# Ranks of a chunk's tokens from a running sum and three matmuls in place of nine, with a new table of orders, in a recurrence and mixture-of-experts kernel

## The chip, the cores and the metric

The kernel runs on one core of a Trainium2 chip. The metric is device time in microseconds (us) of one execution. TensorE is called PE below, VectorE DVE, ScalarE ACT, GpSimd POOL, and SyncE SP; SP and ACT also issue DMAs.

## The reference

First a gated linear recurrence over 4 sequences of 5056 tokens and 256 features, then a top-1 mixture of 8 experts over all 20224 tokens, all in f32:

```python
a_t = exp(8 * sigmoid(r_gate) * log(sigmoid(a_param)))
x_gated = sqrt(max(1 - a_t * a_t, 1e-06)) * sigmoid(i_gate) * x
h = a_t[:, t] * h + x_gated[:, t]          # over the 5056 tokens; y[:, t] = h

logits = y @ w_gate                        # 256 x 8
e_idx = argmax(logits, axis=1)
probs = softmax(logits)
eom = sigmoid(y @ w_output_gate)
for e in range(8):                         # for the tokens with e_idx == e
    ye = relu(y[mask] @ w1[e]) @ w2[e]     # 256 x 1024, 1024 x 256
    out[mask] = probs[mask, e] * eom[mask, e] * ye
```

## The kernel before

The tokens form 158 tiles of 128, in 21 chunks: two chunks of 4 tiles, then 8 tiles each, the last of 6. For each chunk SP loads r, i and x (512 KB each for 4 tiles); ACT makes tanh (L665, L668), exponential (L675), square (L679) and root (L684); DVE the products and the scan along the tokens (L719). ACT and DVE cut the states into two f16 halves (L879, L886). PE makes the logits (L903).

Then comes the routing of the chunk, in `chunk`. ACT takes an exponential (`chances`, L946) and DVE writes the one-hot rows `oh` of each token's expert (`chosen`, L954). PE counts, for each token, the earlier tokens of the same expert (`ranks`, L957): one matmul of `oh` with a strict triangle of ones (`before`, L960) ranks a token within its tile, and one matmul with all ones for each tile adds up the tiles ahead of it and leaves the chunk's counts in the last 8 columns (L962). Those are nine matmuls for 8 tiles and seven for 6. DVE makes positions from them (`positions`, L993), ACT an exponential of the output gate (`outer`, L974), and POOL scatters the tokens' rows to each expert's region in DRAM (L456, one DMA for each tile). The regions have 2 x 128 rows of zeros ahead of the tokens, written by two DMAs of 1.056 MB from `fill` (L443).

Slots of 128 or 256 rows of one expert are then fetched back transposed (L1135, L1136) and go through both layers: PE (L1207, or L1193 for the first seven slots, with plain f32 weights), relu on ACT (L1232, or L1228), the low half on DVE (L1235), PE (L1282, or L1268), scale on ACT (L1303), store by POOL (L1306). Slots 0 to 63 have 128 rows, 64 to 103 have 256, and 19 more of 128 rows end the program. Layer 1 and 2 of expert e are weight units u = 2e and 2e + 1 (1 MB each). A unit is loaded (L512; units 0 to 6 by ACT's queue, the rest by SP's), then a Gram matrix on PE (L538, tile `pg`), its squares on ACT (L544, `dg`), the total on PE (L547) and bits on DVE (L552) give its scale; ACT writes the high halves (L580), DVE the low halves (L590). Units 14 and 15, those of expert 7, pass through a small ring (`fw`) in quarters of chunk size.

The order on PE, ACT and DVE is fixed when the program is built: `in_order` (L120) simulates a list of works with estimated times, takes on each engine the ready work of least rank, and the ranks are tables of numbers (UNIT_RANK, CHUNK_RANK, SLOT_RANK, QUICK, EARLY and so on); LAG and SLACK are two of its estimated delays. SP's and POOL's instructions are kept in their order by dependencies that `queue` adds.

Of the kernel before, what the change touches and what calls it, by code (L numbers as in the profile page):

```python
# [8 lines left out]
F16 = mybir.dt.float16  # L9
# [26 lines left out]
SPLITS = {"S": "ACT", "D": "DVE"}  # L36
SCALED = {"ACT": 1.02, "DVE": 0.7}
# [17 lines left out]
LAG = 0.00147  # L55
ALONE = (0, 1, 3, 6)
QUICK = 37.49
ROOT = -7.725
EARLY = -480.236
UNIT_RANK = (120.607, 156.984, -22.135, -57.114, -38.444, 290.958, -25.836, -53.543, -351.66, -60.25, -83.269, 204.06, -49.573, 717.572, -49.486, -48.406)  # L60
CHUNK_RANK = (-34.925, -64.277, 238.262, 167.391, 124.285, 43.855, 232.134)
SLOT_RANK = (150.646, 149.964, -116.729, -108.112, -120.454)
FILL = 86.095
LOAD_RANK = -320.944
# [10 lines left out]
TABLES = 685.603  # L75
# [4 lines left out]
ROWS_RANK = 755.631  # L80
STEP_RANK = (199.167, -77.575, -71.806, 126.108, -14.56, 59.572, 718.133, -82.438, -33.277, -97.55, -14.479, 318.871, 153.875, -14.556, -57.371, 29.933, -73.206, 178.593, -312.846, 318.846, 312.183, 742.276, 184.836, 99.928)
LOW_RANK = (191.252, 201.868, 132.459, 143.811, -381.683, 24.21, 205.805, 69.861, 69.687, 171.968, 205.098, 132.255, -8.661, 194.752, 178.288, 130.17)
GRAM_RANK = (143.381, -100.9, -76.264, -83.834, -14.807, -100.812, -47.002, -95.429, 247.785, -101.987, -46.114, 82.179, -257.24, -102.206, -102.521, 35.209)
LOGIT_RANK = -206.354
LOAD_AFTER = (0, 0, 1, 1)
WEIGHTS_BY = 'AAAAAAASSSSSSSSS'
SLACK = (0.0, 0.309)
# [164 lines left out]
def rglru_moe(ctx: ExitStack, tc: tile.TileContext, x, r_gate, i_gate, a_param, wg, wog, w1, w2, out, shape):  # L252
# [29 lines left out]
    wide = min(c for c, w in SETS.items() if w > P)  # L282
    add_slots(NC - 1, ENDS + GROUP, P)
# [116 lines left out]
    )  # L400
    ids = const.tile([P, CH], F32, name="ids")
# [86 lines left out]
    def unit(u, staged):  # L488
# [86 lines left out]
        for k in range(1 if i and g == 1 else 2):  # L575
            t = 2 if i and g == 1 else 1

            def by_scale(engine, dst, fw):
                if engine == "ACT":
                    nc.scalar.activation(dst, fw, AF.Copy, scale=s)  # L580
                else:
                    nc.vector.tensor_scalar(dst, fw, s, None, op0=ALU.mult)
# [5 lines left out]
            def lo(k=k):  # L588
                d, fw = cut()[k]
                nc.vector.scalar_tensor_tensor(d[:, 1], fw, s, d[:, 0], op0=ALU.mult, op1=ALU.subtract)  # L590
# [4 lines left out]
            if LOWS[u] == "D":  # L595
                ends.append(work("DVE", t * 1.15 + 0.05, lo, [w], rank + LOW_RANK[u], uses=parts))
                continue
            if k == 0:
                dw = work("DVE", 0.15, scaled_identity, [scaled], -9)
            for v in range(2 * t):  # L600
# [17 lines left out]

                m = work("PE", 1.1, take, [w, dw, pold], rank + LOW_RANK[u], uses=[pu] + parts)
                ends.append(work("ACT", 0.54, give, [m], rank + LOW_RANK[u], uses=[pu]))  # L620
# [11 lines left out]
    def chunk(c):  # L632
# [315 lines left out]
        def chosen():  # L948
            eq, mx, oh = st("eq", E), st("mx", 1), st("oh", E, F16)
# [73 lines left out]
        quick = rank + QUICK  # L1023
# [402 lines left out]
```

## Time and profile before

| | before |
|---|---|
| median of 3 runs (lowest to highest) | 1015.27 us (1010.53 to 1015.96) |
| profiled execution, time | 1015.02 us |
| profiled execution, span | 1013.3 us |
| granted clock of PE, mean | 0.986 |
| PE busy | 941.1 us, 93% |
| DVE busy | 681.7 us, 67% |
| ACT busy | 618.0 us, 61% |
| POOL busy | 345.6 us, 34% |
| chain that ended last | PE 64%, issue 13%, DMA 8%, DVE 6%, ACT 5%, POOL 3% |

The span is the profiler's, from the first to the last instruction; the execution took 1.7 us more. A row of the views gives a start and a duration in us or ns, and the instruction by the line of the kernel before. PE's matmuls overlap, so a matmul's own duration is longer than its place on PE: the place is read from start to start.

### The profile page before, as it was taken

How to read it: one execution, taken by the hardware profiler on the slowest of the kernel's cores; microseconds unless marked ns; L12 is line 12 of the kernel's file. 1: busy time of each engine (PE TensorE's matmuls, PEld its weight loads, DVE VectorE, ACT ScalarE, POOL GpSimd, SP SyncE). 2: the span in 40 equal slices, each digit the busy share in tenths (PEclk: the TensorE clock that was granted, in tenths of full speed). 3: DMA queues.
4: the chain of work that ended last, by engine and by line, in shares of the span. 5: the costliest groups of instructions: out<-in, count | busy, mean ns of one | idle time of the engine just before them, and what ended most of it. 6: DMA issues, size and time to landing. Idle time of an engine off the chain costs nothing.

```text
span 1013.3 us, 27790 instructions
## 1 busy us (share of the span) xinstructions
PE 941.1 (93%) x10820; PEld 862.8 (85%) x10820; DVE 681.7 (67%) x1718; ACT 618.0 (61%) x929; POOL 345.6 (34%) x339
## 2 busy tenths in 40 slices
PE   1389958999999999999999999999999999999996
PEld 1279947999999899998888888888888888899996
DVE  5779999988988798888888888786222222222321
ACT  8779998886776777686768787732322223223332
POOL 1202353344445444444344434453211212121111
PEclk9989978999999999999999999999999999999999
DMA  9999678999999999999988798667212222137771
GB/s 332 388 315 236 175 226 213 217 195 204 216 248 192 241 213 234 189 226 224 226 208 218 198 233 218 141 132 222 58 53 53 53 54 44 46 110 250 225 229 44
DMA packets 269703, 189.96 MB, mean 187 GB/s; under 512 B 211548, under 2 KB 222558, under 8 KB 269568
## 3 DMA queue, kind: packets, MB, share of 16 engines
q1 hardware_dynamic: 249904, 138.57, 59.4%
q0 software_dynamic: 15456, 42.22, 13.2%
q10 hardware_dynamic: 4208, 7.34, 2.0%
q8 instruction: 88, 1.44, 0.6%
q14 instruction: 47, 0.39, 0.1%
HBM read 79.09 MB, written 45.02 MB: 122 GB/s over the span
## 4 chain that ended last, share of the span: by engine, by line
PE 64%; issue 13%; DMA 8%; DVE 6%; ACT 5%; POOL 3%; SPq 0%; POOLq 0%; ACTq 0%; DVEq 0%
PE ph L1207 29%; PE po L1282 28%; DMA xt<-xs 3%; DMA it<-in_i_gate_dram 2%; POOL out_dram L1306 2%; PE ph L1193 2%; DMA w1r<-in_moe_w_dram 2%; DMA rt<-in_r_gate_dram 1%; DVE h L1235 1%; PE lg L903 1%; DVE it L719 1%; PE pg L538 1%; PE po L1268 1%; DVE peak L771 1%; DMA out_dram<-ot,osc 1%
## 5 line engine op out<-in xcount | busy, mean ns | idle before, releaser
L1282 PE MATMUL po<-w2r,h 128*128 128x256 f16 (+1 forms) x3744 | 517.6, 273 | 3.7 <-DVE w2r L590 1.8
L1207 PE MATMUL ph<-xt,w1r 128*128 128x128 f16 (+1 forms) x4656 | 454.3, 242 | 10.0 <-DVE h L1235 3.2
L1207 PEld LDWEIGHTS <-w1r 128*128 128x128 f16 x4656 | 362.7, 98 | 40.0 <-issue 4.2
L1282 PEld LDWEIGHTS <-h 128*128 128x128 f16 x3744 | 346.1, 98 | 40.1 <-issue 5.7
L1235 DVE SCALAR_TENSOR_TENSOR h<-ph,h 128x512 f16<-128x512 f32 x312 | 206.4, 684 | 231.9 <-ACT h L1232 227.8
L1306 POOL DMA_INDIRECT out_dram<-ot,osc x163 | 167.8, 1030 | 397.9 <-ACT ot L1303 349.7
L1232 ACT ACTIVATE h<-ph 128x512 f16<-128x512 f32 x312 | 177.7, 592 | 193.8 <-PE po L1282 175.1
L456 POOL DMA_INDIRECT xs<-rows_all,posi x158 | 174.2, 1103 | 255.9 <-ACT h L1232 87.9
L1303 ACT ACTIVATE ot<-po,osc 128x256 f32<-128x256 f32 x163 | 72.3, 469 | 126.7 <-PE po L1282 63.6
L719 DVE TENSOR_TENSOR_SCAN it<-rt,last,it 128x512 f32<-128x512 f32 (+4 forms) x78 | 94.6, 1238 | 0.3
L1207 PE MATMUL ph<-xt,ws 128*128 128x128 f16 x912 | 69.5, 219 | 0.0
L1207 PEld LDWEIGHTS <-ws 128*128 128x128 f16 x912 | 60.5, 98 | 2.6
L687 DVE SCALAR_TENSOR_TENSOR it<-it,xt 128x1024 f32<-128x1024 f32 (+1 forms) x40 | 48.3, 1207 | 20.7 <-ACT it L684 20.7
L675 ACT ACTIVATE rt<-rt,lam 128x512 f32<-128x512 f32 (+1 forms) x80 | 61.2, 802 | 0.5
L886 DVE SCALAR_TENSOR_TENSOR rt<-it,scale,rt 128x512 f16<-128x512 f32 (+1 forms) x76 | 50.3, 702 | 11.8 <-ACT rt L879 11.5
L671 DVE SCALAR_TENSOR_TENSOR xt<-it,xt 128x1024 f32<-128x1024 f32 (+1 forms) x40 | 48.3, 1208 | 7.5 <-ACT it L668 7.4
L668 ACT ACTIVATE it<-it 128x1024 f32<-128x1024 f32 (+1 forms) x40 | 41.7, 1043 | 11.4 <-DMA it<-in_i_gate_dram 8.0
L665 ACT ACTIVATE rt<-rt 128x1024 f32<-128x1024 f32 (+1 forms) x40 | 41.8, 1044 | 10.0 <-DMA rt<-in_r_gate_dram 7.9
L679 ACT ACTIVATE it<-rt 128x1024 f32<-128x1024 f32 (+1 forms) x40 | 41.8, 1044 | 6.7 <-DVE xt L671 4.6
L684 ACT ACTIVATE it<-it,quarter 128x1024 f32<-128x1024 f32 (+1 forms) x40 | 45.1, 1135 | 0.3
L879 ACT ACTIVATE rt<-it,scale 128x1024 f16<-128x1024 f32 (+1 forms) x38 | 41.1, 1131 | 5.8 <-DVE scale L793 5.7
L771 DVE TENSOR_REDUCE peak<-it 128x1 f32<-128x1024 f32 (+1 forms) x34 | 39.5, 1195 | 0.0
(181 smaller groups left out, 674.3 us busy)
## 6 DMA issues: line engine op xcount, KB each, us to landing
rt<-in_r_gate_dram SPq DMA_DIRECT2D x39, 512.0 KB
it<-in_i_gate_dram SPq DMA_DIRECT2D x39, 512.0 KB
xt<-in_x_dram SPq DMA_DIRECT2D x39, 512.0 KB
ws<-w1r SPq DMA_DIRECT2D x38, 512.0 KB
w1r<-in_moe_w_dram ACTq DMA_DIRECT2D x4, 1024.0 KB
w2r<-in_moe_w_dram SPq DMA_DIRECT2D x4, 1024.0 KB
w2r<-in_moe_w_dram ACTq DMA_DIRECT2D x3, 1024.0 KB
w1r<-in_moe_w_dram SPq DMA_DIRECT2D x3, 1024.0 KB
```

Of the source, the lines that this page charges most:

```text
L456: op = nc.gpsimd.indirect_dma_start(out=xs[:, :], out_offset=bass.IndirectOffsetOnAxis(ap=pos, axis=0), in_=rows.bitcast(F32), in_offset=None,
L671: nc.vector.scalar_tensor_tensor(t("xt"), t("it"), 1.0, t("xt"), op0=ALU.add, op1=ALU.mult)
L675: nc.scalar.activation(r[:, h], r[:, h], AF.Exp, scale=lam[:, h:h + 1], bias=lam[:, h:h + 1])
L719: nc.vector.tensor_tensor_scan(H[:, h, lo:hi], A[:, h, lo:hi], H[:, h, lo:hi], first, op0=ALU.mult, op1=ALU.add)
L771: nc.vector.tensor_reduce(tiles["peak", c][:, b // 4:b // 4 + 1], tiles["it", key][:, :, 0:m], axis=AX.XY, op=ALU.max, apply_absolute_valu ...
L886: nc.vector.scalar_tensor_tensor(halves(key, 1, m // P)[:, :, h], of_tiles(key, m)[:, :, h], tiles["scale_of", c], halves(key, 0, m // P)[ ...
L1207: nc.tensor.matmul(ph[:, i, 0:w], lhsT=ws[:, f // 2 % 2, a, c, f % 2 * P:(f % 2 + 1) * P], rhs=xt[:, b * ND + c, 0:w], start=k == 0, stop= ...
L1232: newest["relu"] = nc.scalar.activation(part(0, f0), tiles["ph", s, f0][:, :, 0:w], AF.Relu).ins
L1235: nc.vector.scalar_tensor_tensor(part(1, f0), tiles["ph", s, f0][:, :, 0:w], 0.0, part(0, f0), op0=ALU.max, op1=ALU.subtract)
L1282: nc.tensor.matmul(po[0:pw, j], lhsT=hh[:, a, f % 4, j * P:j * P + pw], rhs=second(b), start=f + j + a + b == 0, stop=f == NF - 1 and a == ...
L1303: nc.scalar.activation(ot[0:pw], tiles["po", s][0:pw, j], AF.Copy, scale=tiles["osc", s][0:pw, j, 0:1])
L1306: op = nc.gpsimd.indirect_dma_start(out=out[:, :], out_offset=bass.IndirectOffsetOnAxis(ap=tiles["osc", s][0:pw, j, 1:2].bitcast(I32), axi ...
```

## The change

From the ninth chunk on (`c >= SUMS`, SUMS = 8) `ranks` issues three matmuls. `chosen` stores `oh` with the experts outermost and the tiles innermost, and a new scan on DVE writes `up`, the running sum of `oh` over the tiles of each expert (a factor of 0 in `later` starts each expert anew). All ones times `up` counts the tokens of all tiles up to and with the token's own, and `not_after`, the triangle minus one, takes the tokens of its own tile off that do not stand before it. A third matmul of 8 columns leaves the counts.

```diff
+    not_after = const.tile([P, P], F16, name="not_after")
+    nc.vector.tensor_scalar(not_after, before, -1.0, None, op0=ALU.add)
+    later_tile = {}
+    for n in sorted({n for _, n in chunks}):
+        t = const.tile([P, E * n], F16, name=f"later{n}")
+        nc.vector.memset(t, 1.0)
+        nc.vector.memset(t.rearrange("p (e j) -> p e j", e=E)[:, :, 0:1], 0.0)
+        later_tile[n] = t
...
         def chosen():
+            if c >= SUMS:
+                tiles["oh_flat", c] = small.tile([P, E * CH], F16, name=f"oh_{c}", tag="oh", bufs=1)
+                tiles["oh", c] = tiles["oh_flat", c][:, 0:E * nt].rearrange("p (e j) -> p j e", e=E)
...
+            if c >= SUMS:
+                up = tiles["up", c] = small.tile([P, E * CH], F16, name=f"up_{c}", tag="up", bufs=1)
+                flat = tiles["oh_flat", c][:, 0:E * nt]
+                nc.vector.tensor_tensor_scan(up[:, 0:E * nt], later_tile[nt], flat, 0.0, op0=ALU.mult, op1=ALU.add)
...
         def ranks():
             pk = tiles["pk", c] = ps_r.tile([P, 512], F32, name=f"pk_{c}", tag="ps_r")
+            if c >= SUMS:
+                up = tiles["up", c][:, 0:E * nt].rearrange("p (e j) -> p j e", e=E)
+                to = pk[:, 0:nt * E].rearrange("p (j e) -> p j e", e=E)
+                nc.tensor.matmul(to, lhsT=not_after, rhs=st("oh", E), start=True, stop=False, skip_group_check=True)
+                nc.tensor.matmul(to, lhsT=ones16, rhs=up, start=False, stop=False, skip_group_check=True)
+                nc.tensor.matmul(pk[:, nt * E:(nt + 1) * E], lhsT=ones16, rhs=up[:, nt - 1], start=False, stop=True, skip_group_check=True)
+                return
...
-        cn = work("DVE", 0.66, chosen, [ch, ex], quick)
+        cn = work("DVE", 0.66 + 0.25 * (c >= SUMS), chosen, [ch, ex], quick)
         pu, pold = rings["ps_r"].new()
-        pk = work("PE", 0.35, ranks, [cn, pold], EARLY + c / 100, uses=[pu], slack=SLACK[c > 4])
+        pk = work("PE", 0.2 if c >= SUMS else 0.35, ranks, [cn, pold], EARLY + c / 100, uses=[pu], slack=SLACK[c > 4])
```

All ranks of the planner change with it, of which two lines stand here; options that the diff also adds (a third engine for the splits, a second round of plain slots) are off by their constants.

```diff
-LAG = 0.00147
+LAG = 0.0016
...
-FILL = 86.095
-LOAD_RANK = -320.944
+FILL = -141.26
+LOAD_RANK = 12.085
...
-SLACK = (0.0, 0.309)
+SLACK = (0.0, 0.517)
```

On every engine the order is new. Three places follow.

SP, at the start of the program (`rt_4`, `xt_4`, `it_4` are loads of the second half of chunk 2, those with `_0` first halves; `xs` is the DRAM tensor of the expert regions). Before:

```order
12 L659 DMA xt_0_188<-in_x_dram 128x2x512
13 L659 DMA rt_4_190<-in_r_gate_dram 128x2x512
14 L443 DMA xs<-zrow 128x8x264
15 L659 DMA xt_4_211<-in_x_dram 128x2x512
16 L659 DMA rt_0_224<-in_r_gate_dram 128x2x512
17 L659 DMA it_4_263<-in_i_gate_dram 128x2x512
18 L659 DMA xt_0_266<-in_x_dram 128x2x512
```

With the change:

```order
12 L677 DMA xt_0_199<-in_x_dram 128x2x512
13 L455 DMA xs<-zrow 128x8x264
14 L677 DMA rt_4_235<-in_r_gate_dram 128x2x512
15 L455 DMA xs<-zrow 128x8x264
16 L677 DMA xt_4_245<-in_x_dram 128x2x512
17 L677 DMA rt_0_278<-in_r_gate_dram 128x2x512
18 L677 DMA it_4_335<-in_i_gate_dram 128x2x512
```

Both zero fills now stand here; before, the second one stood 281 rows further down, between loads of chunk 11.

ACT, at the start (`w1r` and `w2r` are weight units, `dg` belongs to a unit's Gram matrix; `rt_0`, `it_0` with 138 to 152 and 149 to 161 are chunks 0 to 2). Before:

```order
L361 ACTIVATE ln_low<-a_base 128x2
L512 DMA w2r<-in_moe_w_dram 128x8x256
L668 ACT_TABLE_LOAD
L668 ACTIVATE it_0_140<-it_0_140 128x1024
L665 ACTIVATE rt_0_144<-rt_0_144 128x1024
L675 ACTIVATE rt_0_138<-rt_0_138,lam 128x512 x2
L679 ACTIVATE it_0_140<-rt_0_138 128x1024
L684 ACT_TABLE_LOAD
L684 ACTIVATE it_0_140<-it_0_140,quarter 128x1024
L668 ACT_TABLE_LOAD
L668 ACTIVATE it_0_146<-it_0_146 128x1024
L512 DMA w1r<-in_moe_w_dram 128x2x1024
```

With the change:

```order
L365 ACTIVATE ln_low<-a_base 128x2
L524 DMA w1r<-in_moe_w_dram 128x2x1024
L524 DMA w2r<-in_moe_w_dram 128x8x256
L686 ACT_TABLE_LOAD
L686 ACTIVATE it_0_151<-it_0_151 128x1024
L693 ACTIVATE rt_0_149<-rt_0_149,lam 128x512 x2
L683 ACTIVATE rt_0_155<-rt_0_155 128x1024
L697 ACTIVATE it_0_151<-rt_0_149 128x1024
L702 ACT_TABLE_LOAD
L702 ACTIVATE it_0_151<-it_0_151,quarter 128x1024
L556 ACTIVATE dg_237,sq_238<-pg_216 128x128
L524 DMA w1r<-in_moe_w_dram 128x2x1024 x2
```

Two weight units instead of one are asked for first, and chunk 1's gate `it_0_146` no longer follows chunk 0's root: a unit's `dg` and more weight loads do. On PE the Gram matrices of units 0 and 1 now stand ahead of chunk 0's logits, where before they stood behind the ranks of chunk 1.

ACT, at the weights of expert 7 (`h` of L1232 or L1264 is the relu of a slot: 7 for `h_0_1569`, `h_1_1701`, `h_0_1572` and `h_1_1752`, 8 for `h_0_1761` and `h_1_1764`; `w2r<-fw` are the halves of unit 15; `it`, `rt` of L668 to L684 and `it` of L686 are chunk 5). Before:

```order
L1232 ACTIVATE h_0_1569<-ph_0_1512 128x4x128
L675 ACTIVATE rt_4_1389<-rt_4_1389,lam 128x512 x2
L544 ACTIVATE dg_1615,sq_1616<-pg_1579 128x128
L668 ACTIVATE it_4_1557<-it_4_1557 128x1024
L580 ACTIVATE w2r<-fw_0_1449,wsc 128x1024
L580 ACTIVATE w2r<-fw_1_1519,wsc 128x1024
L946 ACTIVATE ex_1664<-df_1653,inv_1500 128x64
L679 ACTIVATE it_4_1557<-rt_4_1389 128x1024
L684 ACT_TABLE_LOAD
L684 ACTIVATE it_0_1262<-it_0_1262,quarter 128x1024
L1232 ACTIVATE h_1_1701<-ph_4_1550 128x4x128
```

With the change:

```order
L1264 ACTIVATE h_0_1572<-ph_0_1519 128x4x128
L897 ACTIVATE rt_0_899<-it_0_726,scale_1558 128x4x256
L897 ACTIVATE rt_4_981<-it_4_1170,scale_1558 128x4x256
L556 ACTIVATE dg_1622,sq_1623<-pg_1582 128x128
L592 ACTIVATE w2r<-fw_0_1463,wsc 128x1024
L592 ACTIVATE w2r<-fw_1_1526,wsc 128x1024
L686 ACTIVATE it_4_1648<-it_4_1648 128x1024
L1264 ACTIVATE h_1_1752<-ph_4_1565 128x4x128
L1264 ACTIVATE h_0_1761<-ph_0_1626 128x4x128
L1264 ACTIVATE h_1_1764<-ph_4_1684 128x4x128
L964 ACTIVATE ex_1767<-df_1750,inv_1559 128x64
```

The gate of chunk 5 moved behind the two scalings of unit 15, and slot 7's second relu moved ahead of the root. Both relus of slot 8 are now here: on PE all 48 matmuls of slot 8's layer 1 moved from behind slot 7's layer 2 to a place ahead of it, and SP fetches slot 8 ahead of the two transposes of chunk 4 (L895) instead of behind them.

## Rows read from the trace of the kernel before

**Rows 1.** Windows of the span (window, length, then busy time and instructions).

```profile
core 0: us, PE busy (x) PEld busy (x) DVE busy (x) ACT busy (x) POOL busy (x), PEclk, DMA share, GB/s
0.00:20.00 20.00, 0.00 (x0) 0.00 (x0) 10.23 (x41) 15.96 (x17) 3.53 (x18) 1.00 0.93 319
20.00:72.00 52.00, 29.79 (x256) 26.79 (x257) 39.45 (x120) 38.88 (x59) 8.50 (x8) 0.93 1.08 370
72.00:130.00 58.00, 57.96 (x506) 53.90 (x506) 53.66 (x121) 56.26 (x77) 15.42 (x13) 1.00 0.86 212
130.00:165.00 35.00, 20.41 (x232) 16.50 (x231) 33.15 (x67) 32.38 (x40) 17.36 (x13) 0.76 0.73 185
165.00:675.00 510.00, 504.93 (x6381) 467.03 (x6380) 441.66 (x1080) 379.06 (x550) 227.49 (x214) 1.00 0.94 211
675.00:1013.00 338.00, 328.04 (x3452) 298.62 (x3449) 103.57 (x294) 95.41 (x188) 73.26 (x75) 0.99 0.39 112
325.00:675.00 350.00, 346.67 (x4116) 317.68 (x4113) 299.49 (x725) 254.83 (x374) 154.17 (x148) 1.00 0.91 208
```

**Rows 2.** What PE waited for (line, releaser: us in total, times, longest).

```profile
PE pg L538 <- DMA w1r<-in_moe_w_dram: 9.7, 2, 7.7
PE pk L960 <- DVE oh L954: 7.9, 5, 5.5
```

**Rows 3.** PE in order of time: the ranks of one chunk in the dense stage.

```profile
349.11 0.19 PE L960 MATMUL pk<-oh,before 128*128 128x64 f16 x1 [0.53 <-DVE oh L954]
349.13 0.35 PE L962 MATMUL pk<-oh,ones 128*128 128x64 f16 x8
349.34 0.49 PE L1207 MATMUL ph<-xt,w1r 128*128 128x128 f16 x6
349.67 0.49 PE L1282 MATMUL po<-w2r,h 128*128 128x256 f16 x3
```

**Rows 4.** DVE by shape (count, busy us, mean ns, idle before it).

```profile
L719 DVE TENSOR_TENSOR_SCAN it<-rt,it 128x64 f32<-128x64 f32 x2 | 0.5, 264 | 0.0
```

**Rows 5.** All engines in order of time, from the start to slot 0.

```profile
18.90 0.40 SPq L443 DMA_DIRECT2D xs<-zrow  x1
...
23.86 1.15 ACT L684 ACTIVATE it<-it,quarter 128x1024 f32<-128x1024 f32 x1
...
71.77 1.49 PE L1193 MATMUL ph<-xt,w1r 128*128 128x128 f32 x11 [0.37 <-DVE xt L1177]
```

**Rows 6.** PE in order of time, slot 7's second layer to slot 8.

```profile
151.56 0.27 PE L1282 MATMUL po<-w2r,h 128*128 128x256 f16 x1 [1.49 <-ACT w2r L580]
153.58 1.23 PE L1282 MATMUL po<-w2r,h 128*128 128x256 f16 x5 [1.75 <-DVE w2r L590]
155.42 0.23 PE L960 MATMUL pk<-oh,before 128*128 128x64 f16 x1 [0.62 <-DVE oh L954]
...
158.11 1.91 PE L1282 MATMUL po<-w2r,h 128*128 128x256 f16 x10 [0.46 <-DVE h L1235]
159.85 3.35 PE L1207 MATMUL ph<-xt,w1r 128*128 128x128 f16 x57
```

**Rows 7.** ACT in order of time: unit 15.

```profile
148.59 0.26 ACT L544 ACTIVATE dg<-pg 128x128 bf16<-128x128 f32 x1
148.75 0.19 ACT L544 ACTIVATION_READ_ACCUMULATOR dg<-pg 128x1 f32 x1
149.41 1.06 ACT L668 ACTIVATE it<-it 128x1024 f32<-128x1024 f32 x1 [0.47 <-DMA it<-in_i_gate_dram]
150.37 2.17 ACT L580 ACTIVATE w2r<-fw,wsc 128x1024 f16<-128x1024 f32 x2
```

**Rows 8.** POOL in order of time: first and last scatter of chunk 3.

```profile
130.62 0.97 POOL L456 DMA_INDIRECT xs<-rows_all,posi  x1 [3.21 <-ACT it L684]
...
147.56 2.51 POOL L456 DMA_INDIRECT xs<-rows_all,posi  x1 [2.57 <-ACT h L1232]
```

**Rows 9.** SP in order of time: the fetch of slot 8.

```profile
156.28 1.21 SPq L1135 DMA_TRANSPOSE xt<-xs  x1
```

More of the change, by code (lines that the diff above doesn't have):

```diff
@@ L34 @@
 MODES = 'SSSSSSSSSSSSSSSS'
-SPLITS = {"S": "ACT", "D": "DVE"}
-SCALED = {"ACT": 1.02, "DVE": 0.7}
+SPLITS = {"S": "ACT", "D": "DVE", "G": "Pool"}
+SCALED = {"ACT": 1.02, "DVE": 0.7, "Pool": 1.1}
 SQUARES = 'AAAAAA'
@@ L74 @@
 LAST = 7
-TABLES = 685.603
+AGAIN = ()
+SUMS = 8
+TABLES = -77.094
 DEPTH = 4
@@ L580, in by_scale @@
                     nc.scalar.activation(dst, fw, AF.Copy, scale=s)
+                elif engine == "Pool":
+                    queue("Pool", nc.gpsimd.tensor_scalar(dst, fw, s, None, op0=ALU.mult))
                 else:
@@ L589, in lo @@
                 d, fw = cut()[k]
[L590 removed]
+                if LOWS[u] == "G":
+                    queue("Pool", nc.gpsimd.scalar_tensor_tensor(d[:, 1], fw, s, d[:, 0], op0=ALU.mult, op1=ALU.subtract))
+                else:
+                    nc.vector.scalar_tensor_tensor(d[:, 1], fw, s, d[:, 0], op0=ALU.mult, op1=ALU.subtract)
             over = split[u - 2] + used_raw.get(u, []) if u > 1 else []
@@ L594, in unit @@
             whole.setdefault(u, []).append(w)
-            if LOWS[u] == "D":
-                ends.append(work("DVE", t * 1.15 + 0.05, lo, [w], rank + LOW_RANK[u], uses=parts))
+            if LOWS[u] in "DG":
+                by_low, cost = {"D": ("DVE", t * 1.15 + 0.05), "G": ("Pool", t * 2.3 + 0.2)}[LOWS[u]]
+                ends.append(work(by_low, cost, lo, [w], rank + LOW_RANK[u], uses=parts))
                 continue
@@ L617, in give @@
                     nc.scalar.activation(of(d[:, 1]), ph if i else ph.rearrange("p (q f) -> p q f", q=2), AF.Copy)
-                m = work("PE", 1.1, take, [w, dw, pold], rank + LOW_RANK[u], uses=[pu] + parts)
-                ends.append(work("ACT", 0.54, give, [m], rank + LOW_RANK[u], uses=[pu]))
+                pm = work("PE", 1.1, take, [w, dw, pold], rank + LOW_RANK[u], uses=[pu] + parts)
+                ends.append(work("ACT", 0.54, give, [pm], rank + LOW_RANK[u], uses=[pu]))
         split[u] = ends
@@ L1114, in slot @@
         ready, vuse = planned[s] if expert is None else (counted[c], again_used[c])
-        plain = expert is not None and c == min(SETS) and expert < RAWS
+        plain = expert is not None and (c == first_set and expert < RAWS or c == second_set and expert in AGAIN)
         scaled = None if expert is None or plain else undone[expert]
@@ L1294, in slot @@
             for u, last in ((2 * expert + 2, layer1), (2 * expert + 3, m)):
-                used_raw[u] = [last]
+                used_raw.setdefault(u, []).append(last)
                 for v in whole.get(u, ()):
@@ L1350, in rglru_moe @@
         for s in slots_in[c]:
-            if s < E and min(s + AHEAD, E - 1) not in begun:
+            if s == E - 1 and AGAIN:
+                continue
+            if s == 2 * E - 1 and AGAIN:
+                weights_of(E - 1)
+                slot(E - 1)
+            elif s < E and min(s + AHEAD, E - 1) not in begun:
                 if s + AHEAD < E - 1 or s >= LAST:
```

34 lines of the change are left out of this document (18 added, 16 removed).

## The prediction

> **What bounds the kernel now.** I read the windows first. The reader is to see in [rows 1] that PE sets the time once slot 0 has begun, with two exceptions. It is idle for the first 20 us and for 52.0 - 29.8 = 22.2 us of the next 52, where 370 GB/s flow and the DMA engines are full (share 1.08). From 72 to 130 us it is busy without a gap (57.96 of 58). From 130 to 165 us it is idle for 35.0 - 20.4 = 14.6 us, at a mean granted clock of 0.76, while ACT (32.4) and DVE (33.2 of 35) have hardly a gap. After that it lacks 5.1 us up to 675 us and 10.0 us to the end, part of which is the last store. So time is won by taking work off PE, by shortening the start, or by closing the hole at 130 to 165 us. Work on DVE after 325 us is covered: DVE is busy 299.5 of 350 us there.
>
> Second, the waits of PE and the timelines: 7.9 us for the one-hot rows in five waits, of which one is 5.5 us long at the start [rows 2]; the hole at expert 7, where PE waits in turn for the high half of unit 15, its low half, the one-hot rows of chunk 4 and slot 7's second hidden half (1.49, 1.75, 0.62 and 0.46 us) and gets to slot 8 only at 159.85 us [rows 6]. Slot 0 begins at 71.77 us [rows 5].
>
> **The change, part by part.** The sum is made against the profiled execution's 1015.0 us (span 1013.3), which is 0.25 us under the median of the runs; I leave that difference out.
>
> Ranks. Chunks 8 to 20 are 13, of which twelve lose six matmuls and the last (seven down to three) loses four: 76 matmuls. Nine of them take PE from 349.11 to 349.34 us, 0.23 us or 25.6 ns each [rows 3], so 76 x 25.6 ns = 1.9 us. This lies on PE where nothing covers it. The lower end: two of the three that stay have 64 columns, and could cost as much as the layer-1 matmuls of 128 columns next to them, 0.33 us for six, 55 ns [rows 3]; then a chunk keeps 0.14 and saves 0.09 us, 1.2 us in all. The upper end is 2.0, with the last one's 8 columns for nothing. I take 1.9, since the row measures these very shapes.
>
> Beside that row stands a rule of the Trainium skill, "TensorE: Matmul & The Clock Gate", section "Back-to-back issue gap": a steady stream of weight loads and matmuls of 128 columns is put at about 81 ns a pair there. As an estimate from that page the 76 pairs would be 6.2 us. The 25.6 ns of the row speak against it for these narrow matmuls, and the 55 ns for the wide ones.
>
> The scan. The nearest row is the scan of 64 f32 elements, 264 ns [rows 4]; 13 x 0.26 = 3.4 us on DVE. DVE lacks 50 us of work in the 350 us in which most of these chunks lie, so this costs nothing by itself. It lies ahead of the ranks, though. Where PE is already waiting for the one-hot rows (0.53 us in [rows 3]) each 0.26 us counts, and behind PE's ranks all slot work is queued in fixed order. Of five such waits two are early, one at expert 7 and only two, 0.7 us, after 165 us. Bounds: 0, and 13 x 0.26 = 3.4 us if all were late. The planner now plans the scan in and gives a longer slack, so I take 0. The new constants on DVE are seven small instructions at the very start, where DVE is busy 10.2 of 20 us [rows 1]: 0.
>
> The second zero fill. It is 1.056 MB, formerly issued among chunk 11's loads under a full PE; now it is right behind the first one, which was issued at 18.90 us [rows 5]. At 370 GB/s [rows 1] it takes 2.9 us of DMA engines that are full until slot 0 starts. At its old place it cost nothing, so nothing comes back. One more weight unit, too, is asked for ahead of slot 0's fetch on SP (six for five): another 2.8 us if all its bytes go first. Bounds 0 (ACT, not a load, is what chunk 2 waits for) and 5.7. I take 2.9, since the fill can't be delayed past what follows it and a weight unit only shares the queues.
>
> Weights first. Units 0 and 1 now come ahead, their Gram matrices stand on PE ahead of chunk 0's logits, and on ACT a unit's squares stand ahead of chunk 1's gate. Chunk 1's root, now at 23.86 us [rows 5], moves some 8 us back as I add up what stands ahead of it; in return PE's 9.7 us of waits for a loaded unit [rows 2] and ACT's scalings of the first units come earlier. Both must be done before slot 0 starts, so I count this as 0; the rest of the start is in the bounds above.
>
> Expert 7. Three things move. (a) ACT: between `dg` of unit 15 and its scaling stood a gate that began after a wait of 0.47 us [rows 7]. Now the scaling follows `dg` at once, but two scalings of chunk 4 stand ahead of `dg`. From 148.75 to 150.37 us that gives 1.3 at least; adding the durations of all ACT work ahead of unit 15's scaling in both orders, by the rows of before, gives 3.6 us less. I take 3.6. (b) PE does slot 8's first layer, 48 matmuls of 55 ns [rows 3], in the hole: 2.7 us that no longer stand behind it. For this slot 8 must be there: its rows come from the scatters of chunk 3, begun at 130.62 and ended at about 150 us [rows 8], and it was fetched at 156.28 us [rows 9], behind two transposes. Now its fetch is ahead of them, and the exponential that frees the scatters stands some 9 us of ACT work earlier. (c) Slot 7's second relu now stands ahead of the root, and the ranks of chunk 4 behind slot 9: 0.46 and 0.62 us of waits [rows 6] go. Together 3.6 + 2.7 + 1.1 = 7.4 us. Bounds: 0, and about 12 of the 14.6 us in [rows 1], as the two units must still pass through ACT and DVE. What is late next is ACT and DVE themselves, nearly full there.
>
> Sum: 1015.0 - 1.9 + 2.9 - 7.4 = **1008.6 us**.
>
> **The rivals.** (1) *The hole only moves.* ACT and DVE bind from 75 to 165 us, and slot 8's second layer still needs its relus behind theirs. Then of expert 7's term 0 to 3 us are left: 1015.0 - 1.9 + 2.9 - 1.5 = 1014.5. For it: ACT and DVE are busy over 92% there [rows 1]. Against it: the order there puts the scalings ahead of work that isn't urgent.
>
> (2) *The start gets longer: slower.* Its place is the queue of loads ahead of slot 0. If the fill and the extra unit (5.7 us) and one more unit's 2.8 us, for the early pair, hold up chunk 1 and 2, slot 0 starts 8.5 us later, at 80 us. PE has done the same work by then in either order and is full up to 130 us, so nothing covers it. With nothing won at expert 7 this gives 1015.0 - 1.9 + 8.5 = 1021.6. It decides if slot 0 starts after 77 us and the hole stays above 12 us. For it: 370 GB/s and a full DMA share; against it: PE's idle 22 us there leave other orders, and weights come early at no cost to later ones.
>
> (3) *The hole nearly closes and the start costs nothing:* 1015.0 - 1.9 - 12 = 1001.1. For it: chunk 3's scatter and slot 8 come forward together, and PE could go on to slot 9.
>
> (4) *The ranks gain nothing:* the scan comes late for PE each time, 3.4 us against 1.9; with the rest as forecast, 1008.6 + 3.4 = 1012.0. Only two late waits for one-hot rows speak for it.
>
> (5) *The removed matmuls cost more than their starts show,* as weight loads run beside the slots' own: at 81 ns for 25.6, the sum would be 1008.6 - 4.2 = 1004.4. Between 349.11 and 349.34 us there is no room for it [rows 3]. It is the rule of the page named above.
>
> **How the numbers follow.** Some 0.5% (5 us) is what a measurement of this kernel can tell from no change; the three runs lie 5.4 us apart. So "faster" is under 1010.2 and "slower" over 1020.3. Forecast 0.43, with its own range of 1005 to 1013 (0.32 of it under 1010.2); rival 1 0.20, rival 2 0.17, rival 3 0.14, rival 4 0.04, rival 5 0.02. Faster: 0.32 + 0.14 + 0.02 and a little of rival 1's deeper end, 0.50. Slower: rival 2's 0.17. Same: 0.33. The range goes from rival 3's 1001 to 1020.5, short of most of rival 2.
>
> **What would show it.** Ranks: three matmuls of a chunk within 0.09 us, and no more than about 1 us of waits for them after 165 us. The fill: two rows near 19 us, and slot 0's first matmul between 72 and 77 us. Expert 7: slot 8's first layer ahead of slot 7's second, idle time of PE in the hole about 7 to 9 us, and a dense stage that begins some 4 us earlier than now. The forecast is wrong if slot 0 starts after 77 us, if PE waits in the hole for slot 8 itself, or if a new wait of PE of over 2 us shows up after 165 us.

## The result

The change makes the kernel slower: 1023.71 us (median of 4 runs, 1022.72 to 1024.67) against 1013.63 us, a ratio of 1.0112 with a 95% interval of 1.0093 to 1.0132. The forecast was 1008.6 us with a range of 1001 to 1020.5. The profiled execution took 1022.72 us (its span is 1020.9 us), 7.7 us more than the profiled one of before. On two other chips, measured later, it costs 0.0 and 0.2%; that is told under "Together".

The windows of the profile after, which answer to the first five lines of [rows 1]:

```profile
core 0: us, PE busy (x) PEld busy (x) DVE busy (x) ACT busy (x) POOL busy (x), PEclk, DMA share, GB/s
0.00:20.00 20.00, 2.48 (x18) 2.13 (x18) 10.27 (x48) 12.47 (x15) 3.53 (x18) 1.00 0.92 322
20.00:72.00 52.00, 21.93 (x147) 19.86 (x147) 33.99 (x95) 37.27 (x52) 9.44 (x8) 0.84 1.03 368
72.00:130.00 58.00, 56.15 (x551) 53.46 (x552) 50.68 (x128) 51.30 (x77) 14.16 (x11) 0.94 0.87 204
130.00:165.00 35.00, 24.46 (x232) 21.02 (x230) 32.20 (x53) 27.33 (x33) 15.29 (x12) 0.85 0.56 167
165.00:675.00 510.00, 502.53 (x6266) 464.80 (x6267) 443.64 (x1087) 385.90 (x557) 240.31 (x209) 0.99 0.94 211
```

From 20 to 72 us PE is busy 7.9 us less than before and ACT 1.6 us less, while as many bytes flow (368 GB/s for 370): the order of the loads is another, not their rate. From 130 to 165 us PE is idle for 10.5 us instead of 14.6. After 165 us it is idle for 7.5 us instead of 5.1, although twelve chunks now take three matmuls instead of nine.

Slot 0 begins at 81.43 us, 9.7 us later than in [rows 5]. PE in order of time:

```profile
81.43 0.73 PE L1225 MATMUL ph<-xt,w1r 128*128 128x128 f32 x4
```

This is no matter of one execution: of the profiles below, five with the start of before (before twice, e1, e7a, e7b) have slot 0 at 69.6 to 71.8 us, and five with the changed start (the change three times, e8, e13) at 81.0 to 81.6.

How the lag goes on can be worked out from the records of layers 1 and 2: each record of a matmul counts its columns at 2.4 GHz (twice for f32, whose records of 128 columns start 0.11 us apart, those of f16 0.056), 846 us in all, and one reads when PE has done a given sum of this slot work. The times behind the kernel before's profile, in us:

| slot work done | 0 | 40 | 52 (expert 7) | 62 | 150 | 400 | 840 |
|---|---|---|---|---|---|---|---|
| changed kernel | +9.7 | +10.5 | +3.3 | +11.0 | +10.0 | +6.8 | +7.6 |
| loads behind (e9, below) | +5.8 | +7.7 | +0.5 | +7.0 | +5.9 | +1.7 | +2.6 |

So the start loses 9.7 us. In the hole at expert 7 the lag is 7.2 us less for as long as slot 8 fills it; 10 us of slot work later all of this is lost again, so the hole gives nothing that lasts. The rest of the program takes 3 us off.

Part of what is lost behind the hole is PE's clock. From 165 to 185 us, before and after:

```profile
165.00:185.00 20.00, 19.50 (x284) 18.46 (x284) 17.85 (x42) 17.28 (x22) 9.68 (x10) 1.00 0.89 232
165.00:185.00 20.00, 14.69 (x167) 12.87 (x168) 15.08 (x40) 16.69 (x22) 2.95 (x3) 0.83 0.91 205
```

A granted clock of 0.83 is a third of this stretch at 1.2 GHz, the rest at 2.4; PE had waited 3.50 us before (below), and the first 42 matmuls of slot 9 take 85 ns each there instead of 56. In the kernel before the low clock lies wholly in the hole (0.76 from 130 to 165 us, 1.00 behind it).

**The ranks.** The place of [rows 3], in the changed kernel's first chunk with three matmuls:

```profile
309.73 0.27 PE L987 MATMUL pk<-oh,not_after 128*128 128x64 f16 x1
309.82 0.29 PE L988 MATMUL pk<-up,ones 128*128 128x64 f16 x1
309.94 0.19 PE L989 MATMUL pk<-up,ones 128*128 128x8 f16 x1
309.98 1.22 PE L1239 MATMUL ph<-xt,w1r 128*128 128x128 f16 x19
```

From the first start to that of the next matmul there are 0.25 us. Nine took 0.23. Each of the two wide ones holds PE about 0.1 us: with the experts outermost, they read their 64 columns 16 bytes apart. DVE by shape, one line of the kernel before, then two of the changed one (count, busy us, mean ns, idle before):

```profile
L954 DVE TENSOR_TENSOR oh<-eq,mx 128x64 f16<-128x64 f32 x18 | 4.0, 225 | 0.6
L975 DVE TENSOR_TENSOR oh<-eq,mx 128x64 f16<-128x64 f32 x18 | 6.7, 375 | 0.6
L979 DVE TENSOR_TENSOR_SCAN up<-later,oh 128x64 f16<-128x64 f16 x12 | 3.5, 293 | 0.4
```

The scan takes 293 ns. The one-hot rows, now written with a step in twelve of the 18 chunks of this shape, take 375 ns in the mean instead of 225; if the other six still take 225, the twelve take 450.

**The start.** ACT and SP queues in order of time:

```profile
15.33 0.40 SPq L455 DMA_DIRECT2D xs<-zrow  x1
...
17.95 3.59 ACTq L524 DMA_DIRECT2D w1r<-in_moe_w_dram  x2
21.55 0.45 SPq L455 DMA_DIRECT2D xs<-zrow  x1
30.72 0.38 ACTq L524 DMA_DIRECT2D w2r<-in_moe_w_dram  x1
31.14 1.28 ACT L693 ACT_TABLE_LOAD   x1 [13.96 <-DMA xs<-zrow]
35.10 0.39 ACTq L524 DMA_DIRECT2D w1r<-in_moe_w_dram  x1
...
39.67 1.15 ACT L702 ACTIVATE it<-it,quarter 128x1024 f32<-128x1024 f32 x1
```

ACT stands still for 14 us; its longest wait up to 75 us was 4.2 before. At the head of its queue are weight loads: the first waits until 17.95 us, the second until 21.15 (both in one row), and the third is issued only at 30.72 us. The exponentials of chunk 1 are behind it. What it waits for the built program lists: every DMA of SP and ACT signals on one of eight semaphores in turn, and one that takes a semaphore again waits until the DMA that had it has landed. This load waits for the first zero fill's semaphore (and for that of a weight unit that has long landed):

```
18 L524 DMA w1r<-in_moe_w_dram 128x2x1024 [waits DMAHW5_49,DMAHW3_49]
19 L524 DMA w2r<-in_moe_w_dram 128x8x256 [waits DMAHW6_49,DMAHW0_49]
```

Chunk 1's root comes at 39.67 us, against 23.86 in [rows 5].

**The hole at expert 7.** PE in order of time, where [rows 6] has slot 7's second layer:

```profile
163.15 1.47 PE L1314 MATMUL po<-w2r,h 128*128 128x256 f16 x12
168.12 0.61 PE L1314 MATMUL po<-w2r,h 128*128 128x256 f16 x2 [3.50 <-ACT h L1264]
...
171.12 3.73 PE L1239 MATMUL ph<-xt,w1r 128*128 128x128 f16 x42
174.69 0.19 PE L992 MATMUL pk<-oh,before 128*128 128x64 f16 x1
```

And ACT, SP in the same stretch:

```profile
161.98 0.39 SPq L677 DMA_DIRECT2D it<-in_i_gate_dram  x1
...
166.04 1.06 ACT L686 ACTIVATE it<-it 128x1024 f32<-128x1024 f32 x1 [3.87 <-DMA it<-in_i_gate_dram]
167.00 1.55 ACT L1264 ACTIVATE h<-ph 128x512 f16<-128x512 f32 x3
```

Slot 8's first layer now lies ahead, as planned. Then PE waits 3.50 us for the relu of slot 7's second half. That relu is behind a gate of chunk 5 on ACT, which waits 3.87 us for a load that SP issues only behind the fetches of slots 8 and 9.

### The profile page after: what moved, and what is told of

The parts are those of the page before. It is cut to its first block, busy times and chain, and to the rows that moved or that the text cites. A ratio compares the mean times of both kernels' runs of the same rounds, so it can differ in the third digit from the quotient of the medians.

```text
span 1020.9 us, 27611 instructions
## 1 busy us (share of the span) xinstructions
PE 943.4 (92%) x10744; PEld 866.6 (85%) x10744; DVE 687.6 (67%) x1738; ACT 612.2 (60%) x927; POOL 362.9 (36%) x339
## 4 chain that ended last, share of the span: by engine, by line
PE 60%; DVE 13%; issue 11%; ACT 6%; DMA 5%; POOL 2%; SPq 0%; POOLq 0%; ACTq 0%; DVEq 0%
PE ph L1239 28%; PE po L1314 27%; DVE it L737 3%; DVE h L1267 2%; POOL out_dram L1338 2%; PE ph L1225 2%; DMA xs<-zrow 2%; PE po L1300 1%; DMA it<-in_i_gate_dram 1%; DVE peak L789 1%; PE lg L921 1%; DVE it L705 1%; DVE xt L689 1%; DMA w1r<-in_moe_w_dram 1%; ACT L702 1%
## 5 line engine op out<-in xcount | busy, mean ns | idle before, releaser
L1338 POOL DMA_INDIRECT out_dram<-ot,osc x163 | 181.8, 1115 | 452.2 <-ACT ot L1335 352.7
L1264 ACT ACTIVATE h<-ph 128x512 f16<-128x512 f32 x312 | 177.0, 593 | 170.9 <-PE po L1314 149.4
L468 POOL DMA_INDIRECT xs<-rows_all,posi x158 | 177.6, 1124 | 191.8 <-ACT h L1264 79.2
L686 ACT ACTIVATE it<-it 128x1024 f32<-128x1024 f32 (+1 forms) x40 | 41.5, 1044 | 19.5 <-DMA it<-in_i_gate_dram 19.3
```

Source lines behind the costliest of these rows:

```text
L468: op = nc.gpsimd.indirect_dma_start(out=xs[:, :], out_offset=bass.IndirectOffsetOnAxis(ap=pos, axis=0), in_=rows.bitcast(F32), in_offset=None,
L1264: newest["relu"] = nc.scalar.activation(part(0, f0), tiles["ph", s, f0][:, :, 0:w], AF.Relu).ins
L1338: op = nc.gpsimd.indirect_dma_start(out=out[:, :], out_offset=bass.IndirectOffsetOnAxis(ap=tiles["osc", s][0:pw, j, 1:2].bitcast(I32), axi ...
```

## The experiments

They ran on several chips. On those of the first eight kernels below (through e8) the kernel before takes 1012 to 1013 us, on those of the rest, under "Together", 1035 to 1037 us. Every ratio is to the kernel before on the same chip, with its 95% interval, and only ratios are compared.

### The new ranks with the old order

e1: the changed code with all tables, LAG and SLACK of before (the planner's estimates for the ranks stay those of the change).

> The new ranks (three matmuls and the scan from chunk 8 on) with all tables, LAG and SLACK of the kernel before. Theory (the loss lies in the new order alone, the ranks save PE 1.9 us): slot 0 begins within 1 us of 71.8 us, and the time is 1 to 3 us under the kernel before (ratio 0.997 to 0.999). Rival (the scan delays the ranks, or the three matmuls cost as much as nine): no gain or a loss, ratio 1.002 or more, with new waits of PE for the one-hot rows or the running sum after 300 us. Second rival (the order of before is upset by the new costs of the planner): a loss of over 3 us spread over the chunks after the eighth.

Measured 1.0028 (1.0013 to 1.0043), so the theory is wrong; slot 0 at 69.84 us. The ranks bring no gain, but the order behind chunk 8 differs a little from before's, so this can't tell the two rivals apart. Hence e7a: in addition the old estimates, which makes the order on every engine that of the kernel before.

```diff
-        cn = work("DVE", 0.66 + 0.25 * (c >= SUMS), chosen, [ch, ex], quick)
+        cn = work("DVE", 0.66, chosen, [ch, ex], quick)
...
-        pk = work("PE", 0.2 if c >= SUMS else 0.35, ranks, [cn, pold], EARLY + c / 100, uses=[pu], slack=SLACK[c > 4])
+        pk = work("PE", 0.35, ranks, [cn, pold], EARLY + c / 100, uses=[pu], slack=SLACK[c > 4])
```

> The new ranks in exactly the order of the kernel before on every engine (its tables, and its estimates for the two works, so that nothing else is moved). Theory (with the experts outermost, the three matmuls read their 64 columns 16 bytes apart and take as long as the nine: 0.25 us against 0.24 in the changed kernel's trace): no gain, the time within 2 us of the kernel before, three matmuls of a chunk 0.25 us from start to start. Rival (the scan on DVE makes PE wait at each chunk): over 2 us slower, with new waits of PE for the ranks after 280 us. Second rival (PE is faster at the ranks, and the order of the run with the old tables hid it): 1.5 to 2 us faster.

Measured 1.0029 (1.0011 to 1.0047). Three matmuls take 0.25 us here too. The theory is right that PE gains nothing; the loss, 2.9 us (1.1 to 4.8), is larger than the 2 us it allowed. PE does not wait for the ranks themselves after 280 us, so the first rival as put is wrong, but in this profile it waits 5.3 us for fetched slot rows there, where the first profile of before (second line) has 1.7:

```profile
PE ph L1239 <- DMA xt<-xs: 5.3, 4, 1.7
PE ph L1207 <- DMA xt<-xs: 1.7, 3, 1.0
```

One profile can't carry more: that the longer way from one-hot rows to scatter is what delays the rows fits, and isn't shown. Nor is it shown how the loss is shared between the scan and the stepped writing of the one-hot rows; no run has one without the other.

e7b: the same, but PE reads both operands as they lie and writes the result with a step.

```diff
-                up = tiles["up", c][:, 0:E * nt].rearrange("p (e j) -> p j e", e=E)
-                to = pk[:, 0:nt * E].rearrange("p (j e) -> p j e", e=E)
+                up = tiles["up", c][:, 0:E * nt].rearrange("p (e j) -> p e j", e=E)
+                oh = tiles["oh_flat", c][:, 0:E * nt].rearrange("p (e j) -> p e j", e=E)
+                to = pk[:, 0:nt * E].rearrange("p (j e) -> p e j", e=E)
```

> As the one in the order of before, but the two matmuls of 64 columns read the one-hot rows and their running sum in the order in which they lie, and write the result with a step instead. Theory (it is the step of what PE reads that costs): three matmuls take 0.08 to 0.11 us instead of 0.25 from start to start, PE loses 13 times 0.15 us, and the time is 1 to 2 us under the one that reads with a step. Rival (the step costs as much where the result is written): 0.25 us again and no difference. Second rival (PE does gain, but the chunks bound it by then): 0.1 us on PE and under 0.7 us in the time.

PE in order of time, e7b:

```profile
347.17 0.22 PE L988 MATMUL pk<-oh,not_after 128*128 128x64 f16 x1
347.20 0.25 PE L989 MATMUL pk<-up,ones 128*128 128x64 f16 x1
347.26 0.20 PE L990 MATMUL pk<-up,ones 128*128 128x8 f16 x1
347.31 0.49 PE L1240 MATMUL ph<-xt,w1r 128*128 128x128 f16 x6
```

0.14 us from 347.17 to 347.31, instead of 0.25. So it is the step of the operand read that made the three as slow as nine, though they are not as fast as the theory said (0.08 to 0.11). The time does not show it: 1.0029 (1.0012 to 1.0045), as e7a, where the theory said 1 to 2 us less. 13 x 0.11 = 1.4 us are less than this interval, so the second rival (PE gains, the time doesn't) fits and isn't told apart from noise.

### The start

e3: the second zero fill held at its place of before, by one more dependency on the newest input load.

```diff
+        if r < FILLS - 1:
+            tc.add_manual_dep(
+                op.ins, inputs_at["SP"].ins.name, mybir.DependencyInfo(mybir.DependencyClass.NoSync, mybir.DependencyReason.DATA),
+                reason="order of the engine",
+            )
```

> The changed kernel with the second zero fill held back to its place of before (among the loads of chunk 11); nothing else is moved. Theory (the second fill lengthens the start twice: by 2.9 us of bytes, and because it takes one of the eight semaphores that SP's and ACT's DMAs use in turn, so that ACT's third weight load falls on the semaphore of the first fill and blocks ACT until that lands at 30.7 us): ACT goes on at about 23 us instead of 31, slot 0 begins 5 to 8 us earlier, at 74 to 76 us instead of 81.4, and the time falls by 4 to 8 us. Rival (weights ahead of chunk 1's work are what fills the queues, whatever the fill does): slot 0 begins at 78.5 us or later and the time falls by 3 us at most.

Slot 0 at 76.30 us, 5.1 us earlier. ACT's stall, by its waits up to 80 us:

```profile
ACT L698 <- DMA xt<-in_x_dram: 6.6, 1, 6.6
```

The load now has the semaphore of an earlier input. The start goes as expected within 0.3 us; the time does not: 1.0101 (1.0074 to 1.0129, of four runs), hardly below the change's 1.0112. Its profile has one new wait of PE of 3.7 us for slot rows between 300 and 400 us. e5 tells the bytes from the semaphore: the fill late, and a load of 1 KB, which nothing reads, at its early place.

```diff
+                if key == (2, 4) and k == 0:
+                    spare = const.tile([P, ND, 1], F32, name="spare")
+                    inputs_at["SP"] = queue("SP", nc.sync.dma_start(spare, a_param.rearrange("(c p o) -> p c o", p=P, o=1)))
```

> As the one with the second fill held back, but a load of 1 KB stands at the fill's early place, so that every later DMA has the semaphore that it has in the changed kernel. Theory (the semaphore counts, not the bytes alone): ACT is blocked again until the first fill has landed, at 27 to 31 us, and slot 0 begins within 3 us of the changed kernel's 81.4 us; the time is 0 to 3 us under the changed kernel. Rival (only the fill's bytes count): the same as with the fill held back, within 1 us.

ACT stands still for 14.3 us again, and slot 0 begins at 80.65 us:

```profile
ACT L701 <- DMA spare<-in_a_param_dram: 14.3, 1, 14.3
```

(The inferred name is that of the spare load. In the built program the weight load, issued at 30.59 us, takes the semaphore of the first fill again.) The ratio is 1.0133 (1.0114 to 1.0152), not the 0 to 3 us under the changed kernel that were expected, and its interval overlaps e3's. It is slot 0 and the stall that tell the two apart, not the time: one KB of load in the wrong turn costs slot 0 4.4 us, and the megabyte of zeros behind that 0.8 more.

e4: the kernel before with its second fill moved up.

```diff
-        queue("SP", op)
+        if r == FILLS - 1:
+            queue("SP", op)
```

> The kernel before with the second zero fill moved up to the start, as the change has it; the order of PE, ACT and DVE stays. Theory (bytes of 2.9 us in a start that the loads bind, and another semaphore for every later DMA): slot 0 begins 2 to 6 us later than 71.8 us and the time is 2 to 6 us over the kernel before. Rival (ACT and not the loads sets slot 0's start in this order): no change within 1 us.

Slot 0 at 74.59 us, 2.8 us later than in [rows 5] (the four other profiles of before's order have it at 69.6 to 70.3), and 1.0027 (1.0011 to 1.0042), 2.7 us. That is the number of the 2.9 us of bytes, but ACT in order of time shows another way to it:

```profile
37.81 0.38 ACTq L513 DMA_DIRECT2D w2r<-in_moe_w_dram  x1
38.23 1.06 ACT L680 ACTIVATE it<-rt 128x1024 f32<-128x1024 f32 x1 [5.48 <-DMA xs<-zrow]
```

Here, too, a weight load on ACT's queue has the semaphore of a fill, by the built program the second one's, and the square behind it begins at 38.23 us, in the kernel before at 34.55. So this run does not show that the bytes cost 2.8 us.

e9: the changed kernel with ACT's loads of units 5 and 6 moved behind chunk 0's first routing exponential, in the planner's finished list.

```diff
+        loads = [next(w for w in listed if w.emit.__name__ == "load" and unit_of(w) == [u]) for u in (5, 6)]
+        at = next(w for w in listed if w.emit.__name__ == "chances")
+        for w in loads:
+            listed.remove(w)
+        k = listed.index(at) + 1
+        listed[k:k] = loads
```

> The changed kernel with two of ACT's weight loads (units 5 and 6) moved behind chunk 0's first exponential of the routing; the order is otherwise as it was. Theory (ACT stands still for 14 us because a weight load at the head of its queue waits for a semaphore): ACT goes on at about 21 us instead of 31, chunk 1's root comes at 30 us or earlier instead of 39.7, slot 0 begins 5 us or more earlier than 81.4 us, and the time falls by 3 to 8 us. Rival (the bytes ahead of it bind chunk 1 and 2 anyway): slot 0 begins after 79 us, and the time falls by less than 2 us.

ACT in order of time, e9:

```profile
21.75 1.28 ACT L693 ACT_TABLE_LOAD   x1 [5.02 <-DMA xt<-in_x_dram]
30.72 1.15 ACT L702 ACTIVATE it<-it,quarter 128x1024 f32<-128x1024 f32 x1
```

ACT stalls for 5.0 us instead of 14.0, chunk 1's root is at 30.72 us, slot 0 at 77.57 us (1.2 us later than the theory's latest), and the ratio 1.0061 (1.0039 to 1.0083): half of the loss. This edit shows that the block on ACT's queue cost time on these chips.

### The hole at expert 7

e8: the gate of chunk 5 and its product behind the relus and low halves of slots 7 and 8.

```diff
+        listed.remove(gate)
+        listed.remove(gated)
+        at = listed.index(square)
+        listed[at:at] = [gate, gated]
```

> The changed kernel with one gate of chunk 5 (on ACT) and its product (on DVE) moved behind the relus and low halves of slots 7 and 8; no other instruction is moved. Theory (that gate waits 3.9 us for a load that SP issues only after two fetches, and PE waits 3.5 us for the relu behind it): PE's wait of 3.5 us goes, slot 9's first layer begins 3 to 4 us earlier, and the time falls by 1.5 to 4 us. Rival (the chunks' own work bounds this stretch, so the wait comes back later): the wait goes, and the time falls by less than 1 us.

PE in order of time, e8:

```profile
165.88 1.26 PE L1314 MATMUL po<-w2r,h 128*128 128x256 f16 x10 [0.56 <-DVE h L1267]
166.98 2.51 PE L1239 MATMUL ph<-xt,w1r 128*128 128x128 f16 x42
174.75 0.21 PE L992 MATMUL pk<-oh,before 128*128 128x64 f16 x1 [5.26 <-DVE oh L975]
```

The wait of 3.50 us is gone, slot 9 begins at 166.98 us instead of 171.12, and then PE waits 5.26 us for the one-hot rows of chunk 4 and does its ranks at 174.75 us, where the changed kernel does them at 174.69. The ratio is 1.0105 (1.0076 to 1.0134). By the rows the rival is right that the wait comes back; the interval alone would allow a gain of 3 us. What holds the one-hot rows up is again a load, as SP, ACT and DVE show:

```profile
163.32 1.20 SPq L1167 DMA_TRANSPOSE xt<-xs  x1
165.27 0.39 SPq L677 DMA_DIRECT2D it<-in_i_gate_dram  x1
165.56 0.34 ACT L964 ACTIVATE ex<-df,inv 128x64 f32<-128x64 f32 x1
169.27 2.00 ACT L686 ACTIVATE it<-it 128x1024 f32<-128x1024 f32 x2 [3.37 <-DMA it<-in_i_gate_dram]
171.30 2.36 DVE L689 SCALAR_TENSOR_TENSOR xt<-it,xt 128x1024 f32<-128x1024 f32 x2 [4.29 <-ACT it L686]
```

Chunk 4's exponential, which the one-hot rows need, is done at 165.9 us. But on DVE two products of chunks 5 and 6 stand ahead of them, and wait for gates on ACT, the first of which (chunk 6's) waits for a load that SP issues behind the fetch of slot 10.

### Together, on chips where the kernel before takes 1036 us

e10: both edits of the start. e13: the changed kernel in its order with nine matmuls and no scan. And a second profile of before.

> The changed kernel with both edits at the start: ACT's two weight loads moved behind chunk 0's first routing exponential, and the second zero fill held back to its place of before. Theory (two separate delays, blocked ACT and 2.9 us of bytes): slot 0 begins at 74 to 76 us (81.4 in the changed kernel, 77.6 with the loads alone), and the time is 1 to 3 us under the one with the loads alone, that is 1.003 to 1.005 of the kernel before. Rival (both act on the same wait): slot 0 within 1 us of 77.6 us and the same time.

> The changed kernel in exactly its order on every engine, but with nine matmuls for the ranks and no scan, in all chunks. Theory (three matmuls take PE as long as nine, and DVE 0.5 us more for each chunk, which in the order of before came to 0.3% of the time): 1 to 4 us under the changed kernel, ratio to the kernel before 1.007 to 1.010. Rival (the planner's order counts on the new works, and the part in the order of before was only due to that order): within 1 us of the changed kernel, ratio 1.0105 to 1.012.

> The kernel before, unchanged, for a second profile: how far the late waits of PE (5.1 us of idle time between 165 and 675 us in the first one) differ from execution to execution. If they are a matter of the order alone, the idle time there is within 0.5 us of 5.1; if they hang on the arrival of scattered rows, it differs by 1 us or more.

The kernel before took 1036.27 us here, e10 came out at 0.9991 (0.9962 to 1.0021) and e13 at 0.9997 (0.9978 to 1.0017). Both lie under all that was expected, by theory and rival alike, so these times decide nothing between them. Slot 0 does for e10: at 73.63 us it begins earlier than with either edit alone (77.57 and 76.30), which speaks against the rival of one common wait. The second profile of before begins as the first (slot 0 at 69.93 us), but PE is idle for 17.7 us from 165 to 675 us instead of 5.1, mostly where the profile shows nothing that it waits for (up to 700 us):

```profile
PE ph L1207 <- issue: 8.4, 18, 1.0
PE po L1282 <- issue: 2.5, 6, 0.9
```

[Rows 2] and the same view of the first profile have no such line. The idle time differs by far more than 1 us, but not for scattered rows, as the second answer had it. Why these chips differ is open. The change itself stands beside e10 and e14 (e10 with nine matmuls, in the same order) on two more of them.

> The changed kernel itself, beside the two that follow, on one chip. If its loss does not depend on the chip: 1.009 to 1.013 of the kernel before. If it does (on the chip of the last two comparisons the kernel before took 24 us more, and the changed order with the nine matmuls as long as it): 0.998 to 1.004.

> Again the changed kernel with both edits at the start (ACT's two weight loads later, the second zero fill late), on one chip with the changed kernel. Theory (the start is most of the loss): slot 0 at 73 to 76 us, and 5 to 9 us under the changed kernel. Rival (what the start loses is given back later): less than 3 us under it.

> The one with both edits at the start, in the same order, but with nine matmuls for the ranks and no scan. Theory (the new ranks cost DVE 0.5 us a chunk and give PE nothing): 1 to 3 us under the one with the new ranks, and so within 2 us of the kernel before. Rival (the ranks are neutral): within 1 us of the one with the new ranks.

> The changed kernel once more, to stand beside the next two on one chip. On a chip where the kernel before takes about 1012 us: 1.009 to 1.013 of it. On one where it takes about 1036 us: 0.998 to 1.003.

> The changed kernel with both edits at the start. On a chip where the kernel before takes about 1012 us: 5 to 9 us under the changed kernel, ratio 1.001 to 1.005 (the start is most of the loss). On one of 1036 us: 0.996 to 1.001, as before. Rival: no more under the changed kernel than the loads alone gave, 1.006.

> Both edits at the start and nine matmuls, same order. On a chip where the kernel before takes about 1012 us: 1 to 4 us under the one with the new ranks, ratio 0.998 to 1.002. On one of 1036 us: 0.992 to 0.997. Rival: within 1 us of the one with the new ranks.

> Both edits at the start and nine matmuls, in the new order, once more, to meet a chip where the kernel before takes about 1012 us. There: 0.998 to 1.002 of the kernel before if the start and the ranks are all that the change loses; 1.003 or more if the new order loses elsewhere too. On a chip of about 1036 us: 0.993 to 0.998.

| chip | changed kernel | e10 | e14 |
|---|---|---|---|
| third | | 0.9991 (0.9962 to 1.0021) | |
| fourth | 1.0004 (0.9983 to 1.0025) | 0.9984 (0.9962 to 1.0006) | 0.9942 (0.9921 to 0.9964) |
| fifth | 1.0021 (1.0003 to 1.0039) | 0.9984 (0.9962 to 1.0006) | 0.9962 (0.9937 to 0.9986) |
| sixth | | | 0.9948 (0.9922 to 0.9975) |

On these chips the change costs next to nothing, although slot 0 begins as late as before (81.59 and 81.03 us). Its lag behind the second profile of before falls from 11.5 us at 40 us of slot work to 1.8 at 800, and the unexplained waits are fewer in its profile from the fourth chip:

```profile
PE ph L1239 <- issue: 1.5, 3, 0.8
```

Why the new order loses less to them is not known. The start's edits (0.2 to 0.4%) and the nine matmuls (another 0.2 to 0.4%) have the same signs as on the first chips, but the intervals overlap for each alone; only the two together are clear of noise against the changed kernel. On the fourth chip the start's edits bring 1.0 us by the medians, where their theory said 5 to 9; there the rival holds, that the start's loss is given back later. e14, the new order without its start and without the new ranks, is faster than the kernel before here, by 0.4 to 0.6%. What it does on the chips of the first kind was not measured, so how the 1.1% there splits is open.

## Why the prediction was wrong

**Ranks, -1.9 us: the sign of nothing.** The step that failed is "I take 1.9, since the row measures these very shapes". [Rows 3] measure matmuls whose operand lies column by column. The new ones read 16 bytes apart, and three take 0.25 us where nine took 0.23. Both bounds (1.2 and 2.0; the upper one, as it is described, would be 89 x 25.6 ns or 2.3) missed it. The diff showed the new layout; I read the columns and not the step. The rule that bears on this stands in the Trainium skill, "SBUF — State Buffer", section "Door 1: The DMA port swizzle": SBUF is read in lines of 16 bytes, and each access that crosses to a new line pays; a result written to PSUM with gaps slows a matmul as well. The runs agree with the first half: from start to start 0.09 and 0.12 us with the 16-byte step on the read side (309.73, 309.82, 309.94), against about 0.026 in [rows 3] without any step. With the second half they agree in part: of e7b's two matmuls that write with a step the first takes 0.03 us and the second 0.06. I did not weigh this rule in the prediction.

**Scan, 0 us: mis-sized.** The scan is near its row (293 ns for 264), but the writing of the one-hot rows with a step was missed. DVE's busy time rose by 5.9 us (681.7 to 687.6), and with the order unchanged the new ranks cost 0.29% (e7a), about 3 us of the loss. The sentence that DVE has slack and the cost is 0 does not hold on these chips; through which wait the 3 us come is not shown.

**Zero fill, +2.9 us: the number met once, by luck.** In before's order slot 0 comes 2.8 us later (e4), but there ACT waits 5.48 us for the fill's semaphore, which the term doesn't contain. In the changed order holding the fill back moves slot 0 by 5.1 us, 4.4 of which a 1 KB load in its place gives back (e5). It was not the bytes but the turn.

**Weights first, "I count this as 0": the step that decides.** I added up durations ahead of chunk 1's root, 8 us, and said that the loads had to be done anyway. The root came 15.8 us later, since three weight loads in a row on ACT's queue hold up ACT's own work for 14 us until their semaphores come free; with two of the loads moved back it comes 8.9 us earlier and half of the 1.1% is gone (e9). A wait added by a moved load was not priced, and who is queued behind it (all of chunk 1's arithmetic) not named. On the chips where the kernel before takes 1036 us the same late start is made up for by the end, and why is open.

**Expert 7, -7.4 us: seen, then given back.** By the slot work 7.2 us are gained there. The forecast asked what is late next and answered ACT and DVE, but let the gain stand. All of it is lost right behind: what is late next is a gate's load, which SP issues behind the slot fetches that the change brought forward, and the forecast priced only what those fetches gain. When the first of these waits is removed, the next of the same kind takes its place (e8). Rival 1, "the hole only moves", is what happened here.

**The rivals.** Rival 2 has the right place and nearly the time: slot 0 at 80 us and 1021.6, measured 81.4 and 1023.7. It had 0.17, because I took the 22 us of idle PE there for room. Its mechanism was half right: the fill and the queue of loads, but by blocked ACT rather than by 8.5 us of bytes. The range ended 1 us short of it. Of what would show the forecast wrong, two things came: slot 0 after 77 us, and a new wait of PE of over 2 us that ends after 165 us (3.50, until 168.12).

## What to carry to other kernels

Count a matmul by the step of its operand as well as by its columns: a layout chosen for the engine that writes can cost the engine that reads all that was saved. A DMA at the head of a computing engine's queue is a wait of that engine; before moving loads forward, list what each must wait for, its turn on a shared semaphore included, and what stands behind it. A gain in a hole between two stretches counts only if the work behind the hole comes sooner too: what was moved forward pushes something else back on the queue that it came from.

## What was not expected of the hardware

A matmul of 64 f16 columns read 16 bytes apart holds PE three to four times as long as one that lies together (0.09 and 0.12 us against 0.03). DVE writes the one-hot rows, 64 f16 elements in each partition, in 225 ns when they lie together, and in some 450 with a step (worked out from the mean of 375 over 18 chunks, of which 12 have it). A weight load at the head of ACT's queue kept ACT from its own work for 9.6 of 14 us (21.15 to 30.72), by the built program for its turn on the semaphore of a DMA of zeros. And the same kernel takes 1012 us on some chips and 1036 on others, with PE idle at moments for which the profile names no cause.
